# The second product for the state reads as seven block products, with a new order of all steps

## The chip, the cores and the metric

The kernel runs on one core of a Trainium2 chip. The metric is device time in microseconds (us) for one execution; lower is better. The core's engines run side by side and synchronise by semaphores: TensorE (matrix multiply; in the profile PE, with PEld for its weight loads), VectorE (DVE), ScalarE (ACT), GpSimd (POOL) and SyncE (SP, which here only issues DMA transfers). TensorE writes into PSUM, eight banks of 2 KB for each of 128 partitions; the other data lie in SBUF.

## What is computed

A cross attention between tokens and states, and a two-layer network on its result:

```python
# x: (8, 8, 512, 64) = (B, H, S, D); state: (8, 8, 32, 64)
a  = softmax(scale * x @ state^T);  xread = a  @ state     # tokens read states
a2 = softmax(scale * state @ x^T);  sread = a2 @ x         # states read tokens
attn = concatenate([xread, sread], axis=2)                  # (B, H, 512 + 32, D)
t = attn.transpose(0, 2, 1, 3).reshape(B * 544, 512)        # 4352 rows
h = t @ w_in                                                # w_in: (512, 2048)
g = maximum(h, 0) + alpha * minimum(h, 0)
out = g @ w_out                                             # w_out: (2048, 512), out: float32
```

Of the 544 output rows of each of the eight batch items 512 belong to tokens and 32 to states. The kernel calls the 8 x 32 = 256 state rows together "the reads" and gives them the item number 8.

## The kernel before

All matmuls are in float16 with float32 sums. The eight items of 512 tokens run one after the other, overlapped; the reads come at the end, because they need the attention of all items.

Every step is a token in one long list, ORDER, and a loop calls the step's function for each. Each engine runs its own instructions in the order in which the list issues them, so the list is the order of all engines. The tokens that matter (b is the item, 8 the reads):

- `F.b.jc.k`: first product, 128 of the 2048 columns of h, into PSUM bank k (0 to 5; two more banks form one larger buffer). For items 0 to 7 two matmuls with 512 columns, for the reads four with 256. `N.b.jc` is ScalarE's relu(-h), `G.b.jc` VectorE's multiply-add that makes g from it and h and so frees the bank.
- `S` and `O`: second product and its copy out for item 0, 16 matmuls of 128x512 for each 128 rows.
- `T`, `A`, `P`, `Q`: second product of items 1 to 7 by Strassen's scheme. The 512 tokens are cut into two halves r, the 2048 rows of w_out into two halves k, its 512 columns into two halves d. Seven products of blocks (`P.b.p.c.k`, p from 1 to 7, c a quarter of it) stand in place of eight. They need sums of blocks of w_out (`T`, once) and, in each item, of blocks of g: `A.b.i.grp.e`, four sums i in two groups of columns, on GpSimd (e = p), on VectorE (v) or by a DMA that adds (d, issued by GpSimd). Three chains of products accumulate in PSUM: p1, then 6, 7 and 4 on top of it; p2; and p5, then 3 on top of it. `Q.b.name.e` takes blocks out: p1, p5 and u are copies of a chain at some point of its way, c11, c12, c21 and c22 are blocks of the output.
- `M`, `MO`: product 2 of item 7 in three pieces, each with its own store.
- `R.q.jc2.k`, `RO.q.e`: second product of the reads. Two groups q of 128 rows, eight steps each, of two matmuls of 128x512, and a copy to SBUF.
- `W...`: a store, issued by SyncE. Stores and SyncE's other transfers start in the order of the list.
- `m`, `mo`, `rd`, `rdo`, `sc`, `sb`, `smax`, `ssh`, `sexp`, `ssum`, `snorm`, `wb`, `tx`, `te`, `tsum`, `tn`, `tt`: the attention. `rdo.b` copies the states' read of one item into the input of the reads' first product.

In the list of before the reads' second product begins while the last F steps are still going on, and its steps are spread over the last products of items 6 and 7:

```python
R.0.1 N.8.10 G.7.15 P.7.1.3 R.0.2 G.8.13 Q.7.p1.a A.7.1.1.d P.6.4.3 G.8.10 F.8.15.1 A.7.2.1.p
...
W.RO.0 M.7.2.0.3 R.1.7 Q.7.c21.a M.7.2.1 RO.1.a W.Q.7.c21 M.7.2.2 M.7.2.3 W.RO.1 MO.7.2.v W.MO.7.2
```

The functions `token_sum_of`, `product`, `token_cols`, `block_rows` and `product_out` already have branches for b == B (item 8) that the list of before doesn't reach: one tile of 128 rows in place of two, blocks of four items each as r, and `parts` in one small tile.

Of the kernel before, what the change touches and what calls it, by code (L numbers as in the profile page):

```python
# [9 lines left out]
F16 = mybir.dt.float16  # L10
# [40 lines left out]
xd.5 tn.3.0.a P.1.4.2 P.1.3.3 te.4.0 P.1.4.3 G.2.7 te.4.1 A.2.1.0.d F.2.15.0 Q.1.c12.v P.2.1.2
Q.1.c21.a A.2.3.1.p P.2.2.0.5 G.2.13 N.2.15 m.4.2 tn.3.1.a tsum.4 m.4.3.4.1 wb.3 P.2.2.1 mo.4.3.a.1
tt.3 P.2.1.3 mo.4.3.a.0 A.2.2.0.p G.2.15 P.2.2.2 mo.4.2.a.1 F.3.6.3 smax.4 W.Q.1.c12 F.3.15.1 N.3.6
P.2.2.3 W.Q.1.c21 mo.4.2.a.0 F.3.1.4 G.3.6 W.Q.1.c22 A.2.2.1.p Q.2.p1.a F.3.3.0 N.3.1 m.4.1
Q.2.c11.v N.3.15 F.3.7.3 G.3.1 P.2.6.0 W.Q.2.c11 mo.4.1.a.0 F.3.9.5 N.3.7 G.3.15 A.2.1.1.d P.2.6.1
N.3.3 G.3.7 ssh.p.4 F.3.0.4 P.2.6.2 G.3.3 N.3.0 P.2.5.0.1 N.3.9 G.3.0 F.3.8.3 mo.4.1.a.1 P.2.6.3
# [12 lines left out]
F.4.6.1 snorm.p.5 Q.3.p5.a F.4.13.3 mo.5.1.v.0 N.4.6 P.3.7.1 mo.5.1.a.1 G.4.8 P.3.3.0 N.4.13 P.3.7.2
G.4.6 A.4.3.0.p F.4.10.2 G.4.13 P.3.7.3 N.4.10 sc.6 Q.3.c22.v rd.4.5 wb.5 m.6.2.1.3 rdo.4.a P.3.3.1  # L70
mo.6.2.a.1 xd.7 P.3.4.0 mo.6.2.a.0 G.4.10 F.4.7.5 P.3.3.2 tx.6 A.4.2.0.p F.4.12.1 P.3.3.3 N.4.12
F.5.9.3 Q.3.c12.v ty.6 N.4.7 P.4.1.0.2 G.4.12 P.3.4.1 te.6.0 W.Q.3.c12 A.4.1.0.d P.4.1.1 G.4.7
te.6.1 tt.5 F.5.8.0 sb.6 P.3.4.2 N.5.9 A.4.3.1.p F.5.3.1 N.5.8 P.4.1.2 N.5.3 G.5.9 P.3.4.3 P.4.1.3
G.5.8 Q.3.c21.a F.5.10.5 A.4.2.1.p Q.4.p1.a smax.6 W.Q.3.c21 m.6.3 N.5.10 P.4.2.0.3 W.Q.3.c22
# [6 lines left out]
snorm.p.6 P.4.3.1 Q.4.c22.v N.5.15 F.5.6.4 W.Q.4.c22 G.5.15 P.4.3.2 N.5.6 P.4.4.0 G.5.4 te.7.0
P.4.3.3 A.5.1.0.d G.5.6 P.4.4.1 A.5.2.0.p m.7.2 Q.4.c12.v m.7.3.1.5 P.4.4.2 mo.7.3.a.1 tsum.7 wb.6
F.5.13.4 F.5.14.3 N.5.13 A.5.3.1.p P.5.1.1 mo.7.3.a.0 G.5.13 P.4.4.3 N.5.14 P.5.1.2 smax.7 F.6.3.1
P.5.2.0.5 N.6.3 F.6.10.4 G.5.14 ssh.p.7 Q.4.c21.a P.5.1.3 G.6.3 mo.7.2.a.1 P.5.2.1 N.6.10 F.6.7.3
Q.5.p1.v F.6.5.2 N.6.7 mo.7.2.v.0 A.5.1.1.d P.5.2.2 tn.7.1.a G.6.7 F.6.14.1 A.5.2.1.p tn.7.0.a
P.5.2.3 G.6.10 m.7.0 N.6.14 rd.6.3 tt.7 Q.5.c11.v sexp.7 P.5.6.0 G.6.14 A.5.4.0.p F.6.8.4 W.Q.5.c11
rdo.6.v P.5.6.1 N.6.8 W.Q.4.c21 F.6.6.5 G.6.8 P.5.6.2 W.Q.4.c12 N.6.6 P.5.5.0.1 A.5.4.1.p N.6.5
G.6.6 P.5.6.3 F.6.4.3 G.6.5 Q.5.u.a F.6.13.4 mo.7.0.a.0 ssum.7 P.5.5.1 N.6.13 P.5.7.0 P.5.5.2
F.6.2.5 G.6.13 snorm.p.7 P.5.7.1 mo.7.0.v.1 F.6.9.2 P.5.7.2 N.6.9 P.5.5.3 N.6.2 G.6.9 P.5.7.3
Q.5.p5.a F.6.11.4 G.6.2 N.6.4 m.7.1 rd.7.2 wb.7 P.5.3.0 rdo.7.a N.6.11 F.6.0.5 G.6.4 P.5.3.1  # L90
mo.7.1.a.1 Q.5.c22.v F.8.6.2 A.6.3.1.p P.5.3.2 G.6.11 N.8.6 F.6.1.3 N.6.0 G.8.6 P.5.4.0 mo.7.1.a.0
G.6.0 F.8.5.4 N.6.1 F.8.2.2 G.6.1 P.5.3.3 N.8.2 F.6.12.5 G.8.2 A.6.3.0.p P.5.4.1 Q.5.c12.v N.6.12
# [22 lines left out]
def kernel(  # L115
# [50 lines left out]
    live = {}  # L166
# [653 lines left out]
```

## Time and profile before

| | |
|---|---|
| time, median of 3 runs | 213.17 us (211.84 to 213.94) |
| the profiled execution | 213.67 us, of which the span from its first to its last instruction 211.8 us |
| mean granted TensorE clock | 0.987 |
| busy: TensorE, VectorE, ScalarE, GpSimd | 202.6, 174.0, 146.1, 170.3 us |
| DMA | 27.09 MB, mean 128 GB/s |

In the lines below, PE is a TensorE matmul, PEld a weight load, DVE VectorE, ACT ScalarE, POOL GpSimd, SPq the queue of transfers that SyncE issues and ACTq that of ScalarE. L655 is line 655 of the kernel: the matmul in `product`; L515 and L524 are the first products, L565 the step G, L547 N, L632 the sum in `token_sum_of`, L686, L690 and L693 the three ways out in `product_out`, L704 and L715 the pieces M and MO, L756 and L766 the reads' second product and its copy, L575 a store. A group line gives the operation, output and inputs with their sizes, the count, busy time in us and the mean in ns of one, and then the idle time of the engine ahead of it and what ended that.

### The profile page before, as it was taken

Reading aid. Unit: us, or ns where it says so; the run is one execution under the profiler, and the core shown is the slowest. Engines: PE = TensorE matmul, PEld = TensorE weight load, DVE = VectorE, ACT = ScalarE, POOL = GpSimd, SP = SyncE. Lnnn points to the kernel's source line nnn. Section 1 sums busy time; section 2 is a strip of 40 time slices with the busy share of each in tenths; the row PEclk is TensorE's granted clock in tenths of the full one; section 3 lists DMA queues with packets and bytes.
Section 4 is the critical chain, followed back from the end, with each engine's and each line's share of the span. In section 5 each row is a group of like instructions: output and inputs, shape, how many; then the busy total and the mean of one; then the engine's idle time right before and its main releaser. Section 6 shows DMA issues by size and latency. Waiting matters only on the chain.

```text
span 211.8 us, 5045 instructions
## 1 busy us (share of the span) xinstructions
PE 202.6 (96%) x2004; PEld 134.0 (63%) x2004; DVE 174.0 (82%) x268; ACT 146.1 (69%) x292; POOL 170.3 (80%) x110
## 2 busy tenths in 40 slices
PE   7689999999999999999999999999999999999992
PEld 6555344444547775676667757766777777877871
DVE  1688998999999999999999999899889876743230
ACT  4188996699997899977987767769667785331002
POOL 7469958999999999998998999999847944499300
PEclk9789999999999999999999999999999999999998
DMA  6999999599958748372998764243900640046026
GB/s 146 175 204 206 207 201 168 54 174 241 203 100 176 125 78 250 58 93 94 189 167 137 159 157 99 53 99 58 194 3 0 160 88 3 0 119 183 0 87 211
DMA packets 44502, 27.09 MB, mean 128 GB/s; under 512 B 22064, under 2 KB 41920, under 8 KB 44480
## 3 DMA queue, kind: packets, MB, share of 16 engines
q0 software_dynamic: 14192, 12.03, 37.6%
q1 hardware_dynamic: 29872, 14.43, 29.4%
q10 hardware_dynamic: 416, 0.33, 0.5%
q8 instruction: 15, 0.25, 0.5%
q14 instruction: 7, 0.06, 0.1%
HBM read 17.31 MB, written 8.91 MB: 124 GB/s over the span
## 4 chain that ended last, share of the span: by engine, by line
PE 81%; DVE 4%; ACT 4%; POOL 4%; DMA 3%; issue 1%; POOLq 0%; ACTq 0%
PE p L655 38%; PE h L515 23%; PE o L581 5%; PE h L524 3%; PE o L756 3%; PE m_ps L482 3%; DVE gp L565 3%; DMA st<-in_state_dram 3%; POOL s L632 2%; PE sr_ps L457 2%; ACT m L504 2%; POOL gp L614 1%; PE sc L322 1%; PE st_ps L256 1%; PE o L704 1%
## 5 line engine op out<-in xcount | busy, mean ns | idle before, releaser
L547 ACT ACTIVATE neg<-h 128x512 f32<-128x512 f32 (+1 forms) x144 | 80.1, 598 | 29.6 <-PE h L515 18.8
L565 DVE SCALAR_TENSOR_TENSOR gp<-neg,oma_sb,h 128x512 f16<-128x512 f32 x128 | 89.5, 734 | 8.0 <-ACT neg L547 7.4
L515 PE MATMUL h<-aT,m 128*128 128x512 f16 x250 | 69.8, 379 | 0.4 <-DVE gp L565 0.3
L632 POOL TENSOR_TENSOR s<-gp,s 128x1024 f16<-128x1024 f16 x28 | 65.8, 2436 | 4.2 <-DVE gp L565 4.0
L655 PEld LDWEIGHTS <-gp 128*128 128x128 f16 x432 | 41.7, 98 | 17.2 <-issue 2.3
L632 POOL TENSOR_TENSOR s<-gp 128x1024 f16<-128x1024 f16 x14 | 32.9, 2350 | 12.0 <-DVE gp L565 12.0
L655 PEld LDWEIGHTS <-s 128*128 128x128 f16 x336 | 31.9, 98 | 13.0 <-POOL s L632 1.6
L655 PE MATMUL p<-ws,s 128*128 128x256 f16 x224 | 33.7, 273 | 0.3 <-POOL s L632 0.2
L655 PE MATMUL p<-ws,gp 128*128 128x256 f16 x224 | 33.6, 273 | 0.0
L515 PEld LDWEIGHTS <-m 128*128 128x128 f16 x250 | 23.9, 98 | 13.5 <-issue 2.2
L504 ACT CAST m<-m_ps 128x512 f16<-128x512 f32 x51 | 28.9, 613 | 4.0 <-PE m_ps L482 2.7
L655 PE MATMUL p<-w_out_sb,gp 128*128 128x256 f16 x208 | 30.3, 273 | 0.0
L367 POOL TENSOR_TENSOR ts<-ts,mx 128x1024 f32<-128x1024 f32 (+1 forms) x9 | 17.1, 1899 | 7.0 <-DVE mx L361 7.0
L383 POOL TENSOR_TENSOR an<-ts,r 128x1024 f16<-128x1024 f32 (+1 forms) x9 | 16.7, 1853 | 2.3 <-DVE r L378 2.3
L581 PE MATMUL o<-w_out_sb,gp 128*128 128x512 f16 x64 | 16.8, 380 | 0.1
L655 PE MATMUL p<-w_out_sb,s 128*128 128x256 f16 x112 | 16.8, 273 | 0.0
L614 POOL DMA_DIRECT2D gp<-gp x14 | 13.6, 972 | 0.4 <-POOL s L632 0.3
L690 ACT COPY c<-p 128x512 f32<-128x512 f32 x6 | 3.5, 582 | 14.3 <-PE p L655 14.3
L482 PE MATMUL m_ps<-w_in_sb,stT 64*32 64x512 f16 x256 | 12.0, 384 | 0.1
L420 ACT ACTIVATE e<-sc,nb 128x512 f16<-128x512 f32 x16 | 11.0, 694 | 0.5 <-issue 0.5
L693 DVE TENSOR_TENSOR c<-p,p 128x512 f32<-128x512 f32 x13 | 8.9, 682 | 2.6 <-PE p L655 2.3
L581 PEld LDWEIGHTS <-gp 128*128 128x128 f16 x64 | 5.8, 97 | 8.1 <-issue 1.6
(73 smaller groups left out, 248.2 us busy)
## 6 DMA issues: line engine op xcount, KB each, us to landing
out_dram<-c SPq DMA_DIRECT2D x27, 256.0 KB, 2.8
xg<-in_x_dram POOLq DMA_DIRECT2D x7, 512.0 KB, 6.9
gp<-gp POOLq DMA_DIRECT2D x14, 256.0 KB, 4.2
w_in_sb<-in_moe_w_in_dram POOLq DMA_DIRECT2D x4, 512.0 KB, 11.5
w_out_sb<-in_moe_w_out_dram POOLq DMA_DIRECT2D x4, 512.0 KB, 12.8
out_dram<-osb SPq DMA_DIRECT2D x4, 256.0 KB, 4.0
out_dram<-osr SPq DMA_DIRECT2D x2, 256.0 KB, 2.5
x<-in_x_dram SPq DMA_DIRECT2D x1, 256.0 KB, 3.3
```

Source lines behind the costliest of these rows:

```text
L367: engine(e).tensor_tensor(ts, ts, over_blocks(cols(live["mx", b], j, S // N)), ALU.subtract)
L383: engine(e).tensor_tensor(blocks(cols(live["an", b], j, S)), blocks(cols(live["ts", b], j, S)), over_blocks(cols(live["r1", b], j, S // N) ...
L420: nc.scalar.activation(live["e2", b][:, g, :, :], live["sc", b][:, :, :, g, :].rearrange("p r j s -> p (r j) s"), EXP, bias=live["nb", b][ ...
L482: nc.tensor.matmul(t[N * k : N * (k + 1), :], st_head(b, h)[64 * r : 64 * r + 64, :], w_in_sb[64 * r : 64 * r + 64, c, 512 * f : 512 * (f ...
L504: copier(e)(m_tile(b)[:, f, g, :], live["mp", b, f][g])
L515: nc.tensor.matmul(h.rearrange("p (r j s) -> p r j s", r=2, j=2), ms[b][:, f, g, 128 * j : 128 * (j + 1)], weights(b, g), start=(g == 0), ...
L547: nc.scalar.activation(neg, h, RELU, bias=0.0, scale=-1.0)
L565: nc.vector.scalar_tensor_tensor(gt, negs.pop((b, jc)), oma_sb[:, jc : jc + 1], h, ALU.mult, ALU.add)
L581: nc.tensor.matmul(outs[b, q], token_cols(b, jc, q), w_out_sb[:, jc, :], start=(jc == 0), stop=(jc == n_jc - 1),)
L614: nc.gpsimd.dma_start(gp[:, 1, 0], gp[:, 1, 1], accum_op=ALU.add)
L632: engine(e).tensor_tensor(t, x, y, op)
L655: nc.tensor.matmul(chains[chain][:, t, :], lhs, rhs[:, i, :], start=(opens and i == 0 and t == 0), stop=(i == half_k - 1), skip_group_chec ...
```

## The change

The tokens R and RO are gone. The reads take the scheme of items 1 to 7 with half the width: `P.8.1` to `P.8.7` (28 steps of two matmuls of 128x256), eight sums `A.8` of 128x512 elements (six on VectorE, A.8.4.0 and A.8.4.1 on GpSimd), seven steps `Q.8` of 128x256, and four stores of 128 KB in place of two of 256 KB. The last of them, c12 of the reads, is issued by ScalarE's queue through a new token WA.

The list is the same up to `S.0.2.5` (196 tokens) and another from there on: F, N, G, P, A, Q, M and the attention stand in another order, in other banks, and some copies have changed between ScalarE and VectorE (27 `mo`, `Q`, `O` and `rdo` steps in one direction or the other, and three `tn` steps between GpSimd and ScalarE). The number of F, P (items 1 to 7), M, m, rd and sc steps is the same. The last F steps now come ahead of all products of the reads, and the end of the list mixes those with products of item 7:

```diff
-W.RO.0 M.7.2.0.3 R.1.7 Q.7.c21.a M.7.2.1 RO.1.a W.Q.7.c21 M.7.2.2 M.7.2.3 W.RO.1 MO.7.2.v W.MO.7.2
...
+A.7.3.0.p P.6.7.2 A.8.3.0.v N.7.4 P.6.2.0.4 G.7.11 F.7.5.1 P.6.7.3 G.7.4 N.7.5 P.6.2.1 A.8.1.0.v
+A.7.1.0.d P.7.1.0.2 Q.6.c22.v P.6.3.0 A.7.2.0.p P.6.2.2 G.7.5 W.Q.6.c22 F.7.12.3 A.8.3.1.v P.6.3.1
+N.7.12 P.7.1.1 A.7.3.1.p G.7.12 P.8.1.0.1 P.6.4.0 P.6.2.3 P.7.1.2 Q.6.c11.v P.8.1.1 P.6.3.2
+A.8.1.1.v W.Q.6.c11 P.8.1.2 A.7.1.1.d P.7.1.3 A.8.2.0.v A.7.2.1.p P.6.3.3 Q.7.p1.a P.6.4.1 Q.6.c12.v
+M.7.1.0.3 P.8.2.0.4 P.6.4.2 P.8.2.1 P.8.1.3 P.6.4.3 A.8.4.0.p P.7.6.0 Q.6.c21.v P.7.5.0.5 A.7.4.0.p
+Q.8.p1.v M.7.1.1 P.7.6.1 P.8.2.2 M.7.0.0.0 P.8.6.0 P.7.6.2 P.8.2.3 M.7.1.2 A.7.4.1.p P.7.6.3
+Q.8.c11.v M.7.0.1 A.8.2.1.v W.Q.8.c11 Q.7.u.a P.8.6.1 M.7.1.3 M.7.0.2 MO.7.1.v P.7.5.1 W.Q.6.c12
+P.7.7.0 W.Q.6.c21 A.8.4.1.p P.8.6.2 P.7.5.2 W.MO.7.1 P.8.5.0.4 P.8.6.3 P.7.7.1 Q.8.u.a P.7.5.3
+P.8.7.0 Q.7.p5.v P.7.7.2 M.7.0.3 P.8.5.1 P.7.7.3 M.7.2.0.3 P.8.7.1 Q.7.c22.v P.8.5.2 M.7.2.1 P.7.3.0
+MO.7.0.v W.Q.7.c22 P.8.5.3 M.7.2.2 P.7.4.0 Q.8.p5.a W.MO.7.0 P.8.7.2 M.7.2.3 P.7.3.1 MO.7.2.v
+P.7.4.1 W.MO.7.2 P.7.3.2 P.8.7.3 P.7.4.2 Q.8.c22.v P.7.3.3 W.Q.8.c22 P.8.3.0 Q.7.c12.v P.8.4.0
+P.7.4.3 P.8.4.1 W.Q.7.c12 Q.7.c21.v P.8.3.1 P.8.4.2 P.8.3.2 P.8.4.3 W.Q.7.c21 P.8.3.3 Q.8.c21.a
+Q.8.c12.v W.Q.8.c21 WA.Q.8.c12
...
+    def store_by_scalar(*what):
+        nc.scalar.dma_start(*stores.pop(what))
...
-        t = sums[b, i, grp] = moe.tile(
-            [128, 4, half_s], F16, name=f"s{i}_{b}_{grp}", tag=f"s_{grp}", bufs=3
-        )
         if b == B:
-            t = sums[b, i, grp] = t[:, :, :128]
+            k = "sums", i in (2, 4)
+            if k not in live:
+                live[k] = att.tile([128, 2, 2, 4, 128], F16, name=f"s{i}_{b}", tag="ts", bufs=2)
+            t = live[k][:, i in (1, 4), grp]
+        else:
+            t = moe.tile(
+                [128, 4, half_s], F16, name=f"s{i}_{b}_{grp}", tag=f"s_{grp}", bufs=3
+            )
+        sums[b, i, grp] = t
+        if b == B:
             gp = live["gs"].rearrange("p (k g j) (r s) -> p r k g j s", k=2, g=2, r=2)[:, :, :, grp]
...
-        "W": store, "M": last_piece, "MO": last_piece_out,
+        "W": store, "WA": store_by_scalar, "M": last_piece, "MO": last_piece_out,
```

More of the change, by code (lines that the diff above doesn't have):

```diff
@@ L51 @@
[L51 to L56, printed above, removed]
@@ L69 @@
[L69 to L74, printed above, removed]
@@ L81 @@
[L81 to L92, printed above, removed]
```

119 lines of the change are left out of this document (67 added, 52 removed).

## The prediction

> **What bounds the kernel now.** I read the page first, then busy time by stage, then what TensorE waits for, and last the chain and the store queue at the end.
>
> ```profile
> span 211.8 us, 5045 instructions
> ...
> PE 202.6 (96%) x2004; PEld 134.0 (63%) x2004; DVE 174.0 (82%) x268; ACT 146.1 (69%) x292; POOL 170.3 (80%) x110
> ```
> ```profile
> 40.00:100.00 60.00, 59.55 (x635) 37.30 (x632) 58.30 (x83) 53.97 (x112) 58.63 (x35) 1.00 0.74 137
> 100.00:120.00 20.00, 20.00 (x219) 13.61 (x204) 19.36 (x29) 16.64 (x34) 18.45 (x12) 1.00 0.91 162
> 120.00:187.00 67.00, 67.00 (x647) 48.70 (x646) 57.99 (x88) 44.85 (x90) 52.64 (x29) 1.00 0.37 78
> 187.00:207.60 20.60, 20.54 (x167) 15.36 (x164) 7.12 (x14) 3.41 (x8) 10.21 (x7) 1.00 0.41 112
> 207.60:211.80 4.20, 0.00 (x0) 0.00 (x0) 0.26 (x1) 0.23 (x1) 0.00 (x0) 0.74 0.59 208
> ```
> ```profile
> PE p L655 <- POOL s L632: 0.2, 1, 0.2
> PE h L515 <- ACT osb L748: 0.2, 1, 0.2
> ```
>
> In the second fence the columns are the stretch, its length, busy time of PE, PEld, DVE, ACT and POOL, the clock, the DMA engines' busy share and GB/s. From 40 us to the last product TensorE idles 0.5 of 167.6 us (59.55 of 60 and 20.54 of 20.6, the rest full) at clock 1.00. The third fence is everything that TensorE waited for after 40 us: two waits, 0.4 us together. A busy TensorE can still be a slow one, so the rate is needed; the chain of waits gives it, because there a run of matmuls stands with its true length:
>
> ```profile
> 182.25 3.06 PE p L655 x28
> ...
> 202.32 0.86 PE o L756 x4
> ```
> ```profile
> 207.20 0.35 PE o L704 x6
> 207.55 0.02 issue
> 207.57 0.29 DVE osb L715
> ```
>
> One 128x256 product matmul takes 3.06/28 = 0.109 us and one 128x512 matmul 0.86/4 = 0.215: cost goes with columns, and no gap is left for another order to close. So TensorE's amount of work sets the end up to 207.55, and after that the stores do. Two other facts matter: VectorE idles only 2.3 us between 40 and 120 (58.30 of 60, 19.36 of 20), so it is nearly a second bound there; from 187 on it is busy a third of the time.
>
> **The products of the reads.** Removed: 16 steps R of two 128x512 matmuls, 32 x 0.215 = 6.88 us. Added: seven products of eight 128x256 matmuls, 56 x 0.109 = 6.10. Every other TensorE step (F, P for items 1 to 7, M, m, rd, sc) is in both lists in the same number. TensorE: -0.78 us, all of it on the path.
>
> **What the blocks need besides.** Eight sums of 128x512 f16 (six on VectorE, two on GpSimd) and seven evictions of 128x256 for two of 128x512. No f16 sum on VectorE is in this trace. Near rows:
>
> ```profile
> L565 DVE SCALAR_TENSOR_TENSOR gp<-neg,oma_sb,h 128x512 f16<-128x512 f32 x128 | 89.5, 734 | 8.0 <-ACT neg L547 7.4
> ...
> L632 POOL TENSOR_TENSOR s<-gp,s 128x1024 f16<-128x1024 f16 x28 | 65.8, 2436 | 4.2 <-DVE gp L565 4.0
> ...
> L547 ACT ACTIVATE neg<-h 128x256 f32<-128x256 f32 x16 | 6.2, 386 | 8.3 <-PE h L524 8.3
> ...
> L565 DVE SCALAR_TENSOR_TENSOR gs<-neg,oma_sb,h 128x256 f16<-128x256 f32 x16 | 7.4, 478 | 2.8 <-ACT neg L547 2.8
> ...
> L693 DVE TENSOR_TENSOR c<-u,p 128x512 f32<-128x512 f32 x7 | 4.8, 683 | 1.6 <-PE p L655 1.6
> ...
> L313 DVE COPY xT<-xT_ps 128x512 f16<-128x512 f16 x7 | 2.6, 406 | 1.1 <-PE xT_ps L308 1.1
> ...
> L383 POOL TENSOR_TENSOR an<-ts,r 128x512 f16<-128x512 f32 x2 | 2.1, 1050 | 0.6 <-DVE r L378 0.6
> ...
> L715 DVE TENSOR_TENSOR osb<-p,o 128x256 f32<-128x256 f32 x1 | 0.4, 422 | 0.0
> ```
>
> The f16 copy gives 0.41, the f32 sum 0.68; I take 0.5 between them, nearer to the row with the same type: 6 x 0.5 = 3.0 us on VectorE, 2.4 to 4.1 by the ends. The Trainium skill (VectorE: DVE Perf Modes, "The perf-mode tier table") has tensor_tensor on 16-bit SBUF data at twice the f32 rate, 1224 ns for 2048 elements; that makes an estimate of 0.42 for 512, and 2.5 us in sum. No run here shows it.
>
> Three of the six sums stand in the list ahead of the last first-product's G (the step G.7.12), three behind it. What comes behind lies in the stretch from 187 on, where VectorE is free two thirds of the time. There I went through each wait that the blocks add, as TensorE steps between the last matmul that an eviction reads and the first that overwrites its bank:
> - u of the reads (ScalarE): the four matmuls each of P.7.7.1 and P.7.5.3, 8 x 0.109 = 0.87 us, against 0.39 for a 256-wide ScalarE pass. The tightest.
> - c22 of the reads (VectorE): ten matmuls, 1.09 us, against 0.42.
> - p1 of the reads: as much as 21 matmuls of 256 columns, 2.3 us, against 0.42 and a c21 of item 6 (0.68) queued ahead on VectorE.
> - GpSimd: its two sums (1.05 each) stand before A.7.4.0 and behind A.7.4.1. Between the place of A.7.4.1 and the first product that reads it lie 8.6 us of TensorE steps, against 2.4 for the sum itself and 3.5 (one sum of each kind) queued ahead.
>
> All are covered with 0.4 us or more to spare, so I cost them at zero. Should the tightest be held up by other ScalarE work, each eviction of 0.6 us queued ahead of it would cost TensorE 0.39 + 0.6 - 0.87 = 0.1 us.
>
> **The end.** Columns: start, length.
>
> ```profile
> 205.68 0.55 SPq L575 DMA_DIRECT2D out_dram<-c  x1
> ...
> 206.27 0.61 SPq L575 DMA_DIRECT2D out_dram<-osr  x1
> ...
> 207.31 0.54 SPq L575 DMA_DIRECT2D out_dram<-c  x1
> ...
> 207.94 0.58 SPq L575 DMA_DIRECT2D out_dram<-osr  x1
> 208.62 0.54 SPq L575 DMA_DIRECT2D out_dram<-osb  x1
> ```
> ```profile
> out_dram<-osr SPq DMA_DIRECT2D x2, 256.0 KB, 2.5
> ...
> out_dram<-osb SPq DMA_DIRECT2D x2, 64.0 KB, 2.1
> out_dram<-osb SPq DMA_DIRECT2D x1, 128.0 KB, 1.9
> ...
> st<-in_state_dram ACTq DMA_DIRECT2D x1, 64.0 KB, 2.6
> ```
> ```profile
> 0.72 0.43 ACTq L194 DMA_DIRECT2D st<-in_state_dram  x1
> ```
>
> Before, the last piece is ready at 207.57 + 0.29 = 207.86, but SyncE is issuing the store ahead of it and starts on it at 208.62: 0.76 us lost. The span ends 211.80 - 207.55 = 4.25 us behind the last matmul.
>
> After, call the end of the last matmul T. The last two evictions are c12 of the reads on VectorE (T + 0.02 + 0.42 = T + 0.44) and c21 on ScalarE (last matmul at T - 0.22, ready at T + 0.19). SyncE still has c21 of item 7: its last matmul ends at T - 1.3, twelve narrow matmuls before T, VectorE ends its 0.68 at T - 0.6 and SyncE its issue at about T. So c21 of the reads is issued at T + 0.2, and c12 goes on ScalarE's queue, which has nothing else left, at T + 0.46 instead of behind it at T + 0.8. Before, the last issue was at 208.62 - 207.55 = T + 1.07: 0.6 us later. The last store is now 128 KB (1.9) for 64 KB (2.1), behind another of 128 KB. A store by ScalarE's queue isn't in the trace; its issue of a load took 0.43, less than SyncE's 0.54. I take -0.5, with ends of 0 and -0.76. The Trainium skill (DMA: Bandwidth & Descriptors, "Issuing engines are not separate DMA queues") says that issuing from several engines saves only the issuing time and that the transfers share the same 16 DMA engines; the 0.76 us here is such an issuing time, so by it too this is the most there is to win.
>
> **The new order.** The lists agree up to S.0.2.5; behind it all is rearranged. TensorE has at most its 0.4 us of waits to win. To lose there is more, on VectorE. I counted steps up to the place where TensorE's steps behind the shared start add up to 84 us (about 120 us in the span). The same number of G; after has one softmax maximum and one sum with its reciprocals more, two state-read copies more, one output copy and two copies of m fewer:
>
> ```profile
> L504 DVE CAST m<-m_ps 128x512 f16<-128x512 f32 x13 | 8.7, 680 | 0.1
> ...
> L361 DVE TENSOR_REDUCE mx<-ts 128x32 f32<-128x1024 f32 x7 | 8.5, 1211 | 0.0
> ...
> L377 DVE TENSOR_REDUCE r<-ts 128x32 f32<-128x1024 f32 x7 | 8.4, 1206 | 0.2 <-ACT ts L373 0.2
> ...
> L378 DVE RECIPROCAL r<-r 128x32 f32<-128x32 f32 x7 | 2.5, 353 | 0.2
> ...
> L430 DVE RECIPROCAL r<-r 128x2 f32<-128x2 f32 x8 | 1.3, 158 | 0.1
> ...
> L468 DVE CAST XS<-sr_ps 128x128 f16<-128x128 f32 x2 | 0.9, 440 | 0.0
> ```
>
> 1.21 + 1.21 + 0.35 + 0.16 + 0.88 - 3 x 0.68 = +1.8 us, into 2.3 us of idle time. It fits, barely. Idle time that lies ahead of where the work arrives can't be used, and G then comes late to free one of the six banks that F opens, so TensorE waits. I take +0.4 us, ends -0.4 (both waits gone) and +1.8 (none of the idle time of use). From there to 187 after has about 3.6 us more on VectorE (three sums, one G and four of the reads' G at 0.46, three more evictions, one copy; one softmax part fewer) against 9.0 idle: nothing.
>
> **Sum.** -0.78 - 0.5 + 0.4 = -0.9 us. The profiled execution took 213.67 (span 211.8 and 1.9 around it), so 212.8 for such a one; it lies 0.5 above the median, 213.17, which gives **212.3**.
>
> **Rivals.**
> (a) VectorE becomes the bound. If none of its idle time between the shared start and 187 is of use, the 1.8 and 3.6 us both go onto TensorE: 213.2 - 1.3 + 5.4 = 217.3; with the first part alone and half of the second, 215.5. It decides once the additions up to 120 pass 2.3 us or arrive in lumps that hold up the F banks. For it: 96 to 97% busy there. Against: before, VectorE runs as dense and TensorE waits for no G after 40; and the new list takes up a bank behind an F no sooner than the old (the closest are 1.7 us of TensorE steps apart in both, 15 of 127 against 16 of 127 lie under 2.2).
> (b) The end gives nothing: the reads' 256 KB now go out last, with rows half as long, and a store by ScalarE's queue lands later by half a microsecond (the load of 64 KB there took 2.6, stores of 64 KB by SyncE 2.1). -0.78 + 0.4: 212.8. For it: the DMA engines are already 59% busy over the last 4.2 us. Against: the store that ended last, before, had waited 0.76 us for SyncE alone.
> (c) Everything turns out well: -0.78 - 0.76 - 0.4 = 211.2. Half of this case would read as faster by over 1%, because runs of one kernel differ by as much (211.84 to 213.94).
>
> **Chances.** Forecast 0.45, (b) 0.15, (c) 0.22, (a) 0.18. About 1% (2.1 us) is what a measurement of this kernel can tell from no change. Faster by over 1% (below 211.0): half of (c) and a part of the forecast from the spread of runs, 0.20. Slower (above 215.3): most of (a), 0.15. Within: 0.65. Range 210.7 to 215.3: below, (c) with some spread; above, the end of the unknown in the order (+1.8 for +0.4: 213.7) and the lower part of (a).
>
> **What would show it.** TensorE's matmuls of L756 gone and 56 more on L655; the last matmul at 206.8 to 207.5; its waits behind 40 us under 1 us in sum, if any on VectorE's G; the f16 sums at 0.4 to 0.7; the span's end 3.6 to 4.0 us behind the last matmul. Waits of TensorE above 2 us between 60 and 130 would prove (a); an end 4.2 us or more behind the last matmul, (b).

## The result and the profile after

The change makes the kernel slower. Six runs of the new kernel have a median of 217.97 us (217.24 to 219.27), six of the kernel before 213.56 (211.84 to 216.53). The ratio, which leaves disturbed runs out, is 1.0244 with an interval from 1.0208 to 1.0281. The forecast was 212.3, in a range up to 215.3.

The page of the profile after first (the execution took 217.42 us as a whole):

```profile
span 215.6 us, 5114 instructions
...
PE 202.6 (94%) x2028; PEld 136.4 (63%) x2028; DVE 185.4 (86%) x282; ACT 145.2 (67%) x290; POOL 171.2 (79%) x111
```

The lines of the program have moved by a few numbers: L667 is now the matmul in `product`, L518 and L527 the first products, L568 the step G, L644 the sum in `token_sum_of`, L698, L702 and L705 the ways out in `product_out`, L716 and L727 M and MO, L507 the copy `mo`, L423 the exponential `te`, L460 `rd`, L578 a store by SyncE, L581 the one that ScalarE issues (in the lines of before L581 is the step S).

TensorE is as long busy as before and the span is 3.8 us longer, so TensorE waits. VectorE is busy for 11.4 us more than before (174.0), although the change brings it some 3 us of sums and a few evictions. These two lines already say where to look. Next, everything that TensorE waits for from the place where the two lists part (about 34 us) to the end; the columns are the waiting line, what it waits for, us in total, times, and the longest:

```profile
PE p L667 <- DVE c L705: 1.5, 1, 1.5
PE sr_ps L460 <- DMA e2T<-e: 1.2, 1, 1.2
PE h L518 <- DVE gp L568: 0.6, 1, 0.6
PE sc L325 <- ACT m L507: 0.5, 1, 0.5
PE p L667 <- DVE s L644: 0.4, 1, 0.4
PE p L667 <- ACT u L698: 0.4, 1, 0.4
PE m_ps L485 <- ACT e L423: 0.2, 1, 0.2
PE h L518 <- ACT XS L471: 0.2, 1, 0.2
```

Eight waits, 5.0 us, where before had two, 0.4 us. Each of them costs some 0.16 us more than it says, because the end of a matmul is modelled late. The timeline of TensorE shows it (start, length, and in brackets the idle time ahead):

```profile
194.02 0.60 PE L667 MATMUL p<-ws,gp 128*128 128x256 f16 x4
194.46 0.60 PE L667 MATMUL p<-ws,s 128*128 128x256 f16 x4
196.51 0.60 PE L667 MATMUL p<-ws,gp 128*128 128x256 f16 x4 [1.45 <-DVE c L705]
```

A group of four is told as 0.60 long, and the next starts 0.44 after it. So this wait is 196.51 - 194.46 - 0.44 = 1.61, not 1.45.

**One measure for all kernels.** The first 36 us vary from run to run, and there all lists are the same. I take the time from a mark in the shared part, the group of eight matmuls of S, to the end of the last matmul, which the chain of waits gives. It is read from one profile of each kernel. For before the chain shown in the prediction ends its matmuls at 207.55, and the mark is this row of TensorE's timeline:

```profile
37.22 1.89 PE L581 MATMUL o<-w_out_sb,gp 128*128 128x512 f16 x8
```

For after, the mark in the timeline, then the last row of the chain (start, length):

```profile
36.07 1.89 PE L587 MATMUL o<-w_out_sb,gp 128*128 128x512 f16 x8
```
```profile
207.45 4.60 PE p L667 x42
```

Before: 207.55 - 37.22 = 170.33. After: 212.05 - 36.07 = 175.98, which is 5.65 longer. Span: 1.15 less in the start, 5.65 more to the last matmul, 0.70 less behind it, in sum the 3.8 above. The start isn't the change's, and some of it is given back: where the mark comes early, the first of the eight waits to come (for the DMA that transposes e) is longer, 1.2 here and 0.3 in two other runs whose marks lie at 37.4.

### The profile page after: what moved, and what is told of

It is laid out like the page before. It is cut to its first block, busy times and chain, and to the rows that moved or that the text cites. A ratio compares the mean times of both kernels' runs of the same rounds, so it can differ in the third digit from the quotient of the medians.

```text
span 215.6 us, 5114 instructions
## 1 busy us (share of the span) xinstructions
PE 202.6 (94%) x2028; PEld 136.4 (63%) x2028; DVE 185.4 (86%) x282; ACT 145.2 (67%) x290; POOL 171.2 (79%) x111
## 4 chain that ended last, share of the span: by engine, by line
PE 64%; DVE 18%; ACT 6%; DMA 6%; issue 3%; POOL 2%; ACTq 0%; POOLq 0%; DVEq 0%
PE p L667 35%; PE h L518 20%; DVE gp L568 7%; DMA w_in_sb<-in_moe_w_in_dram 4%; DVE s L644 3%; PE m_ps L485 3%; PE h L527 3%; ACT m L507 2%; DMA e2T<-e 2%; ACT e L423 2%; DVE nb L408 2%; DVE m L507 2%; DVE ts L356 1%; DVE c L705 1%; PE sr_ps L460 1%
## 5 line engine op out<-in xcount | busy, mean ns | idle before, releaser
L550 ACT ACTIVATE neg<-h 128x512 f32<-128x512 f32 (+1 forms) x144 | 78.6, 589 | 28.7 <-PE h L518 21.5
L568 DVE SCALAR_TENSOR_TENSOR gp<-neg,oma_sb,h 128x512 f16<-128x512 f32 x128 | 89.1, 736 | 4.8 <-ACT neg L550 4.7
L518 PE MATMUL h<-aT,m 128*128 128x512 f16 x250 | 70.3, 379 | 1.2 <-DVE gp L568 0.9
L644 POOL TENSOR_TENSOR s<-gp,s 128x1024 f16<-128x1024 f16 x28 | 62.5, 2368 | 4.4 <-DVE gp L568 4.1
L667 PEld LDWEIGHTS <-gp 128*128 128x128 f16 x432 | 42.0, 98 | 16.3 <-issue 2.5
L667 PEld LDWEIGHTS <-s 128*128 128x128 f16 x368 | 35.0, 98 | 13.0 <-issue 2.0
L667 PE MATMUL p<-ws,s 128*128 128x256 f16 x248 | 37.2, 273 | 0.9 <-DVE s L644 0.4
L667 PE MATMUL p<-ws,gp 128*128 128x256 f16 x224 | 33.6, 273 | 1.5 <-DVE c L705 1.5
L518 PEld LDWEIGHTS <-m 128*128 128x128 f16 x250 | 23.4, 98 | 15.4 <-issue 3.3
L644 POOL TENSOR_TENSOR s<-gp 128x1024 f16<-128x1024 f16 x14 | 30.3, 2172 | 3.5 <-DVE gp L568 3.2
L507 ACT CAST m<-m_ps 128x512 f16<-128x512 f32 x53 | 30.1, 610 | 3.8 <-DVE m L507 2.6
L667 PE MATMUL p<-w_out_sb,gp 128*128 128x256 f16 x208 | 30.1, 273 | 0.0
L370 POOL TENSOR_TENSOR ts<-ts,mx 128x1024 f32<-128x1024 f32 (+1 forms) x9 | 15.9, 1767 | 8.1 <-DVE mx L364 8.1
L620 POOL DMA_DIRECT2D gp<-gp x14 | 12.7, 926 | 7.1 <-issue 6.3
L667 PE MATMUL p<-w_out_sb,s 128*128 128x256 f16 x120 | 18.2, 273 | 0.0
L423 ACT ACTIVATE e<-sc,nb 128x512 f16<-128x512 f32 x16 | 11.0, 689 | 3.9 <-DVE ts L356 2.1
L408 DVE TENSOR_REDUCE nb<-sc 128x2 f32<-128x1024 f32 x8 | 9.7, 1216 | 1.0 <-PE sc L325 0.9
L705 DVE TENSOR_TENSOR c<-p,p 128x512 f32<-128x512 f32 x13 | 8.9, 681 | 1.9 <-PE p L667 1.2
```

The source lines that it names most:

```text
L370: engine(e).tensor_tensor(ts, ts, over_blocks(cols(live["mx", b], j, S // N)), ALU.subtract)
L408: nc.vector.tensor_reduce(nb, live["sc", b].rearrange("p r j g s -> p g (r j) s"), AX.XY, ALU.max)
L423: nc.scalar.activation(live["e2", b][:, g, :, :], live["sc", b][:, :, :, g, :].rearrange("p r j s -> p (r j) s"), EXP, bias=live["nb", b][ ...
L507: copier(e)(m_tile(b)[:, f, g, :], live["mp", b, f][g])
L518: nc.tensor.matmul(h.rearrange("p (r j s) -> p r j s", r=2, j=2), ms[b][:, f, g, 128 * j : 128 * (j + 1)], weights(b, g), start=(g == 0), ...
L550: nc.scalar.activation(neg, h, RELU, bias=0.0, scale=-1.0)
```

## The experiments

Ten kernels. Times of the kernel before, in the same rounds, had medians from 212.19 to 212.65. "Mark to last matmul" is the measure just explained.

**Is it the new reads or the new order?** First the new reads in the old order: the list of before up to `G.8.14`, R and RO taken out, the block products put into the tail by hand, with all eight sums on VectorE behind `Q.7.p5.v`:

```diff
-W.RO.0 M.7.2.0.3 R.1.7 Q.7.c21.a M.7.2.1 RO.1.a W.Q.7.c21 M.7.2.2 M.7.2.3 W.RO.1 MO.7.2.v W.MO.7.2
...
+P.7.7.0 P.7.5.2 P.7.7.1 P.7.5.3 M.7.0.3 Q.7.p5.v A.8.3.0.v A.8.2.0.v P.7.7.2 M.7.2.0.3 P.7.7.3
+M.7.2.1 Q.7.c22.v P.7.3.0 A.8.3.1.v A.8.2.1.v W.Q.7.c22 P.8.6.0 P.8.6.1 A.8.1.0.v P.7.3.1 A.8.1.1.v
...
+P.8.4.1 P.8.3.2 P.8.4.2 W.Q.7.c21 P.8.4.3 P.8.3.3 Q.8.c21.a Q.8.c12.v W.Q.8.c21 WA.Q.8.c12
```

> The order of before up to P.6.3.2 and G.8.14, and the seven products of the reads in a tail written by hand: all eight f16 sums on VectorE behind Q.7.p5, where GpSimd has just ended its last sum. Theory 1: the sums take 0.4 to 0.5 us each, TensorE waits under 0.6 us behind 185, the last matmul ends near 206.9 and the span 3.6 us behind it: 212.3, 1.2 under before. Theory 3 (the new form of the reads costs more than it saves wherever it stands): 215 or more. Theory 2 (the order alone): also 212.3, so this run speaks against theory 3 only.

Measured: 211.12 us (median; 210.59 to 214.55), ratio 0.9941 [0.9906, 0.9976]: 0.6% faster than the kernel before, with an interval that lies below 1, and faster than the changed kernel. TensorE's waits from 34 us on, the sums' group rows, and the last row of the chain:

```profile
PE p L667 <- POOL s L644: 0.2, 1, 0.2
PE h L518 <- ACT osb L760: 0.2, 1, 0.2
```
```profile
L644 DVE TENSOR_TENSOR s<-gs,s 128x512 f16<-128x512 f16 x4 | 1.6, 420 | 0.1
L644 DVE TENSOR_TENSOR s<-gs 128x512 f16<-128x512 f16 x4 | 1.6, 416 | 0.0
```
```profile
202.57 4.38 PE p L667 x40
```

The waits are those of before, and its mark is at 37.22 too: 206.95 - 37.22 = 169.73, 0.60 less than before. The block products do what the sum said of them (0.78), and the loss isn't theirs.

Then the other way round, the new order with the reads as R and RO:

```diff
-S.0.2.5 F.1.1.0 S.0.0.6 mo.1.3.v.0 N.1.1 F.1.3.5 tn.1.1.a G.1.1 S.0.0.7 lx.3 sc.2 tt.1 O.0.0.a
...
+S.0.2.5 mo.1.3.a.0 F.1.1.0 rd.0.5 N.1.1 G.1.1 rdo.0.a lx.3 tn.1.1.a sc.2 F.1.5.5 tx.2 tt.1 F.1.9.0
```

> The changed kernel's order, with the reads' second product in its old form (16 steps R, no f16 sums of the reads, two evictions and two stores). Theory 1: the waits before 190 us stay (about 3 us: the first states' read for its transpose, first products for VectorE, two for ScalarE), those behind it go: 0.8 more TensorE work, 1.9 less waiting: 216.5 to 217. Theory 2 (all from the order): 218 or more. Theory 3 (all from the sums): 213.5.

Measured: 217.17 us (216.31 to 217.43), ratio 1.0205 [1.0140, 1.0269]. Mark to last matmul 173.22, 2.9 more than before, with the waits of after in the middle (0.7, 0.5, 0.4, 0.2, 0.2) but only 0.3 for the transposing DMA. Its mark lies at 37.41, as late as before's. So the order by itself costs about 3 us, and nearer to 4 when the start is early.

**The sums beside GpSimd.** The six sums on VectorE, by groups, after:

```profile
L644 DVE TENSOR_TENSOR s<-gs,s 128x512 f16<-128x512 f16 x2 | 5.2, 2586 | 0.0
L644 DVE TENSOR_TENSOR s<-gs 128x512 f16<-128x512 f16 x4 | 5.0, 1250 | 0.0
```

10.2 us where the kernel above needs 6 x 0.42 = 2.5. The timeline of VectorE and GpSimd in that stretch:

```profile
186.59 2.41 POOL L644 TENSOR_TENSOR s<-gp,s 128x1024 f16<-128x1024 f16 x1
...
187.61 3.75 DVE L644 TENSOR_TENSOR s<-gs 128x512 f16<-128x512 f16 x1
188.68 2.39 POOL L644 TENSOR_TENSOR s<-gp 128x1024 f16<-128x1024 f16 x1
191.28 0.73 DVE L568 SCALAR_TENSOR_TENSOR gp<-neg,oma_sb,h 128x512 f16<-128x512 f32 x1
...
192.54 0.41 DVE L644 TENSOR_TENSOR s<-gs 128x512 f16<-128x512 f16 x1
192.55 0.86 POOL L620 DMA_DIRECT2D gp<-gp  x1 [1.49 <-issue]
192.87 2.98 DVE L644 TENSOR_TENSOR s<-gs,s 128x512 f16<-128x512 f16 x1
193.16 2.40 POOL L644 TENSOR_TENSOR s<-gp,s 128x1024 f16<-128x1024 f16 x1
195.78 0.68 DVE L705 TENSOR_TENSOR c<-u,p 128x512 f32<-128x512 f32 x1
...
197.04 4.21 POOL L644 TENSOR_TENSOR s<-gp,s 128x1024 f16<-128x1024 f16 x2
...
199.34 2.19 DVE L644 TENSOR_TENSOR s<-gs,s 128x512 f16<-128x512 f16 x1
```

Each long sum ends 0.3 us behind GpSimd's: 187.61 + 3.75 = 191.36 and 188.68 + 2.39 = 191.07; 195.85 and 195.56; 201.53 and 201.25. A sum beside GpSimd's issue of a DMA (192.55) takes its 0.41. The multiply-adds of L568, which read h from PSUM, take 0.73 to 0.74 whatever GpSimd does. And because VectorE is in order, the eviction c12 of item 6 (195.78) stands behind the sum of 2.98, and TensorE's 1.45 behind that.

The theory: a VectorE sum with two inputs in SBUF doesn't run while GpSimd is in its own sums. The rivals: these sums are slow wherever they stand, or VectorE simply has too much to do. Three experiments part them. In the first, ScalarE copies one input of each of the six sums to PSUM (four copies for six sums), and nothing else is moved:

```diff
+        if b == B and e == "v":
+            c = live["cp"][:, grp].rearrange("p (j s) -> p j s", s=128)
+            a21, a22 = (a21, c) if i == 2 else (c, a22)
...
+            live["cp"] = two("cp", [128, 2, 512], F32)
...
+        nc.scalar.copy(
+            live["cp"][:, grp].rearrange("p (j s) -> p j s", s=128), gs[:, 1, k, grp]
+        )
```

> The changed kernel, but ScalarE first copies one operand of each of the six VectorE sums to PSUM (four copies), so that no VectorE sum has two inputs in SBUF. Theory 1 (a VectorE sum with two SBUF inputs can't run while GpSimd runs its own two-input sums): the six sums take 0.7 us each whatever GpSimd does, none over 1 us; TensorE's waits of 1.45 us near 196 and 0.44 near 201 go; time 216.0, 1.9 under the changed kernel. Theory 2 (the sums are late only because the new order is late as a whole): the sums keep durations of 2 us or more, or the waits move to the next step; time 217.5 to 218. Theory 3 (all of the loss comes from the sums): 213.

Measured: 216.87 us (214.89 to 219.13), ratio 1.0167 [1.0073, 1.0260]. The timeline:

```profile
191.11 2.42 POOL L647 TENSOR_TENSOR s<-gp,s 128x1024 f16<-128x1024 f16 x1
...
192.40 0.68 DVE L647 TENSOR_TENSOR s<-gs,cp 128x512 f16<-128x512 f16 x1
...
193.20 2.41 POOL L647 TENSOR_TENSOR s<-gp 128x1024 f16<-128x1024 f16 x1
194.86 0.68 DVE L647 TENSOR_TENSOR s<-cp,gs 128x512 f16<-128x512 f32 x1
```

All six take 0.68, three of them (at 192.40, 194.86 and 201.59) wholly in the midst of GpSimd's sums, and those of 128x1024 are no longer for it (2.40 to 2.42 here, 2.39 to 2.41 in after). The slower form (0.68 for 0.42) is the faster one there. Both waits of the tail are gone (TensorE is busy all the time from 190 to 210). Its profiled run has another wait, 2.36 us for the DMA that adds, at 67.20. The clock then stands at 0.50 until about 70, some 1.4 us more by estimate. So its mark to last matmul, 177.44, doesn't serve as a measure; without these two it would be about 173.5 by the same estimate, near the 173.82 of the next experiment.

The second experiment leaves after's order as it is to `G.7.12` and puts all eight sums behind `Q.7.p5.v`, where GpSimd has ended:

```diff
-A.7.3.0.p P.6.7.2 A.8.3.0.v N.7.4 P.6.2.0.4 G.7.11 F.7.5.1 P.6.7.3 G.7.4 N.7.5 P.6.2.1 A.8.1.0.v
+A.7.3.0.p P.6.7.2 N.7.4 P.6.2.0.4 G.7.11 F.7.5.1 P.6.7.3 G.7.4 N.7.5 P.6.2.1 A.7.1.0.d P.7.1.0.2
...
+W.Q.6.c12 P.7.7.0 W.Q.6.c21 P.7.5.2 W.MO.7.1 P.7.7.1 P.7.5.3 M.7.0.3 Q.7.p5.v A.8.3.0.v A.8.2.0.v
```

> The changed kernel with its order up to G.7.12 as it is, and all eight f16 sums of the reads on VectorE behind Q.7.p5, where GpSimd has ended its last sum; the products that read them come behind. Theory 1 (a two-input sum waits for GpSimd's port; order and sums each have their own share): the sums take 0.42 us each, the waits of 1.45 and 0.44 us go, those ahead of 190 us stay: about 2.1 under the changed kernel, 215.3. If the loss in the tail came from the order too (theory 2): 217 or more.

Measured: 215.55 us (214.98 to 215.95), ratio 1.0138 [1.0093, 1.0184]. The sums take 0.41 to 0.43 (414 to 425 ns), the waits for c and s are gone, the six others are there as before. Mark to last matmul 173.82, 2.16 less than after: what the two waits come to (1.45 + 0.44 + 2 x 0.16 = 2.2).

The third turns it round. In the good kernel (the old order with the new reads) one sum is moved to a place ahead of GpSimd's last row of sums:

```diff
-F.8.15.1 A.7.2.1.p P.8.2.0.5 N.8.15 P.7.6.0 G.8.15 F.8.12.0 Q.6.c21.v P.8.2.1 N.8.12 G.8.12 P.7.6.1
+F.8.15.1 A.7.2.1.p P.8.2.0.5 N.8.15 P.7.6.0 G.8.15 F.8.12.0 A.8.3.0.v Q.6.c21.v P.8.2.1 N.8.12
```

> The old order with the new reads, and one f16 sum (A.8.3.0, 0.42 us of work) ahead of Q.6.c21 on VectorE, where GpSimd runs sums back to back. Theory 1: this sum lasts until GpSimd's row of sums ends, 4 us or more; Q.6.c21 behind it and the piece M.7.1 that needs its bank are late; TensorE waits 3 us or more and the time is 214 or more. If a sum just shares the port: it lasts 0.5 to 1 us and the time stays at 211 to 212.

Measured: 218.21 us, one run. VectorE, GpSimd and TensorE in the timeline, and a stretch of the stages' table (length; PE, PEld, DVE, ACT, POOL busy; clock; DMA share; GB/s):

```profile
189.39 6.55 POOL L644 TENSOR_TENSOR s<-gp,s 128x1024 f16<-128x1024 f16 x3
...
189.83 6.40 DVE L644 TENSOR_TENSOR s<-gs 128x512 f16<-128x512 f16 x1
...
196.88 1.01 PE L716 MATMUL o<-w_out_sb,gp 128*128 128x128 f16 x8 [5.94 <-DVE c L702]
```
```profile
198.00:200.00 2.00, 2.00 (x11) 1.42 (x10) 0.64 (x2) 0.00 (x0) 0.00 (x0) 0.50 0.79 264
```

One sum of 0.42 us takes 6.40, to 0.29 behind the end of three GpSimd instructions in a row, and TensorE waits 5.94 us for the copy queued behind it. The clock is at 0.50 from 194 to 200, so TensorE runs at half speed for 3 us behind the wait: 11 matmuls start in the stretch shown, 21 in the 2 us after it. One moved token costs 7.4 us from the mark to the last matmul (177.14 for 169.73).

**The order.** Two kinds of wait are in after's middle. The first can be read in the timeline around 112 and 126 us:

```profile
110.78 1.25 DVE L356 STREAM_TRANSPOSE ts<-sc 128x1024 f32<-128x1024 f32 x1
...
112.06 0.69 ACT L423 ACTIVATE e<-sc,nb 128x512 f16<-128x512 f32 x1 [1.32 <-DVE ts L356]
...
112.74 0.58 ACT L698 COPY u<-p 128x512 f32<-128x512 f32 x1
...
113.36 0.60 PE L667 MATMUL p<-ws,s 128*128 128x256 f16 x4 [0.42 <-ACT u L698]
...
125.93 1.28 DVE L507 CAST m<-m_ps 128x512 f16<-128x512 f32 x2
126.64 0.58 ACT L507 CAST m<-m_ps 128x512 f16<-128x512 f32 x1 [1.33 <-DVE m L507]
```

ScalarE and VectorE read the same tile of two PSUM banks, one behind the other. ScalarE waits 1.3 us for VectorE's read of the scores and for its copy of m, and what stands behind ScalarE is late: u at 112.74, and then a product. At 46.64 it is VectorE that waits, for 1.08 us, and g of the first product is late by it. The waiting engine stands idle even before the other begins its read: in the last line ScalarE is idle from 125.31 and VectorE's copy starts at 125.93; at 46.64 VectorE is idle from 45.56 and ScalarE's copy starts at 45.99. So it waits for the instruction that stands ahead in the list, and not only while two reads would meet. Where the two halves of m lie in two tiles of one bank each, the copies overlap; the same timeline of before:

```profile
108.42 0.69 DVE L504 CAST m<-m_ps 128x512 f16<-128x512 f32 x1
108.87 0.58 ACT L504 CAST m<-m_ps 128x512 f16<-128x512 f32 x1
```

Before also has copies of m by both engines out of one tile, but 3 to 20 tokens apart in the list; behind the shared part of the list, five of after's six such pairs stand 1 or 2 apart. The experiment puts four of these five (3.1, 5.3, 6.1 and 6.2; not 7.2) on ScalarE alone, and the exponentials of items 4 and 6 ahead of VectorE's read, next to each other:

```diff
-mo.3.1.v.1 F.1.0.3 N.1.7 F.1.6.0 G.1.10 N.1.0 S.0.0.7 G.1.7 N.1.6 F.1.4.5 lx.4 S.0.1.6 sexp.2 G.1.0
+mo.3.1.a.1 F.1.0.3 N.1.7 F.1.6.0 G.1.10 N.1.0 S.0.0.7 G.1.7 N.1.6 F.1.4.5 lx.4 S.0.1.6 sexp.2 G.1.0
...
-A.2.3.0.p te.4.1 P.1.4.1 sb.4 P.1.3.3 N.2.7 W.Q.1.c22 P.1.4.2 te.4.0 tsum.3 P.2.2.1 G.2.4 P.2.1.0.1
+A.2.3.0.p te.4.1 te.4.0 P.1.4.1 sb.4 P.1.3.3 N.2.7 W.Q.1.c22 P.1.4.2 tsum.3 P.2.2.1 G.2.4 P.2.1.0.1
...
-N.4.5 m.6.2 P.3.7.1 N.4.7 W.Q.3.c11 G.4.5 P.3.3.0 N.4.6 A.4.3.0.p P.3.7.2 mo.6.2.v.1 mo.6.2.a.0
+N.4.5 m.6.2 P.3.7.1 N.4.7 W.Q.3.c11 G.4.5 P.3.3.0 N.4.6 A.4.3.0.p P.3.7.2 mo.6.2.a.1 mo.6.2.a.0
```

> The changed kernel; the two copies out of one two-bank PSUM tile are given to ScalarE both (m of 3.1, 5.3, 6.1, 6.2: one VectorE copy each became a ScalarE copy), and the two exponentials of items 4 and 6 both stand ahead of VectorE's transpose of the same tile. Theory 4 (two engines' reads of one PSUM tile run one behind the other, and what is queued behind the waiting engine is late): TensorE's waits at 48 (0.65, first product for VectorE), 113 (0.42, for ScalarE's u) and 127 us (0.54, scores for ScalarE's m) go, about 2 us in all with what the modelled ends hide: 215.4. If VectorE's amount of work were the bound there (my rival a): VectorE has 4 copies of 0.68 less, waits shrink by no more than that and sit in other places; 216 to 217.

Measured: 216.69 us (216.29 to 218.14), ratio 1.0205 [1.0139, 1.0272]. TensorE's waits that answer to it, besides the 1.4 and 0.4 of the sums, which stay:

```profile
PE m_ps L485 <- ACT m L507: 0.6, 1, 0.6
...
PE sr_ps L460 <- DMA e2T<-e: 0.3, 1, 0.3
...
PE h L518 <- DVE gp L568: 0.2, 1, 0.2
```

The waits at 113 and 127 are gone and that for g fell from 0.6 to 0.2, but ScalarE, which now has both copies, makes a new one of 0.6. Mark to last matmul is 1.79 less than after (174.19); 0.95 of that is the shorter wait for the DMA, which isn't the edit's. So the edit is worth about 0.84.

The other kind is that DMA. In before's list four S steps, three F steps and the scores `sc.2` stand between the mark and `rd.0`, in after's one F step; its input, transposed by a DMA issued at 35.49, lands at 39.62. The experiment puts three S steps ahead of it, and leaves `sc.2` behind it:

```diff
-S.0.2.5 mo.1.3.a.0 F.1.1.0 rd.0.5 N.1.1 G.1.1 rdo.0.a lx.3 tn.1.1.a sc.2 F.1.5.5 tx.2 tt.1 F.1.9.0
-T.1.1.p N.1.5 S.0.2.6 N.1.9 sb.2 S.0.3.5 ty.2 S.0.2.7 te.2.1 S.0.3.6 G.1.5 te.2.0 T.2.1.p S.0.3.7
+S.0.2.5 mo.1.3.a.0 F.1.1.0 N.1.1 G.1.1 S.0.2.6 S.0.3.5 S.0.2.7 rd.0.5 rdo.0.a lx.3 tn.1.1.a sc.2
+F.1.5.5 tx.2 tt.1 F.1.9.0 T.1.1.p N.1.5 N.1.9 sb.2 ty.2 te.2.1 S.0.3.6 G.1.5 te.2.0 T.2.1.p S.0.3.7
```

> The changed kernel with the first states' read (rd.0) three second-product steps of item 0 later, which come ahead of it instead. If the 1.2 us that TensorE waited there for the transpose by DMA lie on its path: the wait is 0.3 us or less and the time 217.0. If VectorE is the bound of that stretch: the wait goes and first products wait for VectorE that much longer; time 218.

Measured: 217.11 us (216.88 to 217.47), ratio 1.0214 [1.0141, 1.0288]. The wait for the DMA is 0.5 in place of 1.2, but a new one of 1.06 for VectorE's g stands at 43.33. Nothing is won (mark to last matmul 176.49, 0.5 more than after): the wait has moved to the engine that is next late. Why can be read from VectorE's timeline and the first product behind it:

```profile
40.26 1.22 DVE L408 TENSOR_REDUCE nb<-sc 128x2 f32<-128x1024 f32 x1 [1.46 <-PE sc L325]
...
42.56 0.71 DVE L568 SCALAR_TENSOR_TENSOR gp<-neg,oma_sb,h 128x512 f16<-128x512 f32 x1
...
43.33 0.59 PE L518 MATMUL h<-aT,m 128*128 128x512 f16 x2 [1.06 <-DVE gp L568]
```

VectorE is idle for 1.46 us until the scores come, which TensorE makes behind `rd.0`; then two attention steps of 1.2 us each stand ahead of the multiply-add that frees the bank. In after the same multiply-add is as late behind the scores, but ten matmuls of S cover it; here four are left there, because six have moved ahead of `rd.0`. In before the scores come first (40.83, and `rd.0` at 42.57). That order wasn't tried in the new list.

**All together.** The moved sums and the reads on one engine:

```diff
-mo.3.1.v.1 F.1.0.3 N.1.7 F.1.6.0 G.1.10 N.1.0 S.0.0.7 G.1.7 N.1.6 F.1.4.5 lx.4 S.0.1.6 sexp.2 G.1.0
+mo.3.1.a.1 F.1.0.3 N.1.7 F.1.6.0 G.1.10 N.1.0 S.0.0.7 G.1.7 N.1.6 F.1.4.5 lx.4 S.0.1.6 sexp.2 G.1.0
...
-A.7.3.0.p P.6.7.2 A.8.3.0.v N.7.4 P.6.2.0.4 G.7.11 F.7.5.1 P.6.7.3 G.7.4 N.7.5 P.6.2.1 A.8.1.0.v
+A.7.3.0.p P.6.7.2 N.7.4 P.6.2.0.4 G.7.11 F.7.5.1 P.6.7.3 G.7.4 N.7.5 P.6.2.1 A.7.1.0.d P.7.1.0.2
```

> The changed kernel with both repairs: the f16 sums behind GpSimd's last sum, and reads of one two-bank tile by one engine (or with the exponentials ahead). If the two causes are separate and add up: 2.1 less for the sums, 0.9 less for the tiles, 214.4; TensorE's waits left are the first states' read for its transpose (0.3 to 1.2) and one for a ScalarE copy near 52 (0.6). If they overlap: 215 to 215.5.

Measured: 214.32 us (213.81 to 215.34), ratio 1.0113 [1.0076, 1.0150]. Mark to last matmul 172.82: 3.16 less than after. The wait for the DMA is 0.17 shorter here; the other 2.99 are what the sums (2.16) and the reads (0.84) gave alone. The two causes add up. Then these two and the later `rd.0` (the diffs above):

> As new_order_both, and the first states' read three second-product steps later. Alone, that step moved TensorE's wait to first products (VectorE's G 1.7 us) and won nothing. If that was because VectorE's copy of m stood behind ScalarE's there, which new_order_both has removed: 1 us under new_order_both, 213.4, waits behind 34 us 1.2 in sum. If VectorE's work itself is late there: as new_order_both, 214.4.

Measured: 215.60 us (214.03 to 216.97), ratio 1.0167 [1.0098, 1.0236]. Mark to last matmul 172.98, the same as without the third edit (172.82). The wait for the DMA is gone and one of 1.0 for g stands in its place. The list still loses 3.25 us against the old order (169.73) with all three edits.

**The last store's queue.** In the good kernel the last store goes to SyncE:

```diff
-P.8.4.1 P.8.3.2 P.8.4.2 W.Q.7.c21 P.8.4.3 P.8.3.3 Q.8.c21.a Q.8.c12.v W.Q.8.c21 WA.Q.8.c12
+P.8.4.1 P.8.3.2 P.8.4.2 W.Q.7.c21 P.8.4.3 P.8.3.3 Q.8.c21.a Q.8.c12.v W.Q.8.c21 W.Q.8.c12
```

> The old order with the new reads, the last store on SyncE's queue in place of ScalarE's. By the prediction's sum the issue waits for the store ahead: about 0.3 us later, span end 3.8 to 3.9 us behind the last matmul in place of 3.5. If the transfers set the end: no change.

Measured: 215.63 us, one run, with a wait of 2.1 us at 115.28 for another item's transposing DMA, which the edit doesn't touch; so it is read from its end alone. There the last matmul ends at 209.99 and the span at 213.9, 3.9 later; with ScalarE's queue it is 206.95 and 210.5, 3.55 later. ScalarE's queue is worth 0.35 us in these two profiles.

## Why the prediction was wrong

Two terms failed: the sums on VectorE, put at nothing, cost 2.2 us, and the new order, put at +0.4, cost 3 to 4. The other two came out near what was worked out.

**TensorE's products: right.** -0.78 was taken, -0.60 measured in the old order, where the waits are the same 0.4.

**The end: right.** -0.5 was taken with ends of 0 and -0.76, and 4.25 - 3.55 = 0.70 came. After's last instructions:

```profile
211.85 0.37 ACT L702 COPY c<-p 128x256 f32<-128x256 f32 x1 [4.87 <-PE p L667]
212.07 0.42 DVE L705 TENSOR_TENSOR c<-parts,p 128x256 f32<-128x256 f32 x1 [0.62 <-PE p L667]
212.53 0.65 ACTq L581 DMA_DIRECT2D out_dram<-c  x1
```

The last store is issued 0.04 behind its eviction, 0.48 behind the last matmul (212.05), as worked out (T + 0.46). Its issue takes 0.65; the prediction, from the 0.43 of a load, had expected less than SyncE's 0.54. Rival (b) falls.

**The sums on VectorE: a cost put at nothing.** The prediction said "All are covered with 0.4 us or more to spare, so I cost them at zero." They cost 2.16 us, and by none of the four waits that the prediction had listed: TensorE waits for an eviction of item 6 that is queued behind a sum, and for a sum itself. The duration of one was right where GpSimd stands still (0.41 to 0.43 measured, 0.5 taken). The estimate of 0.42 that the prediction drew from the Trainium skill (VectorE: DVE Perf Modes, "The perf-mode tier table") agrees with it. What failed is the check: I asked whether each eviction's engine is free for as long as its instruction lasts, and took the sum's length as the same everywhere. I counted GpSimd's work only as a chain of its own, not as what VectorE would have to stand aside for, and three of the six sums (3.75, 2.98 and 2.19 us above) lie just where GpSimd makes the last sums of item 7. "VectorE is free two thirds of the time" there was a fact of an engine with no such instruction in it: the trace of before has no f16 sum on VectorE, as the prediction itself said.

The Trainium skill has this rule, and the prediction left it out: GPSIMD Engine Reference, "8. Key points", tells of contention with VectorE instructions that have two SBUF inputs, and SBUF — State Buffer, "SBUF: two separate sides", of an exclusive lock that whichever starts first has for the whole instruction. The traces agree that VectorE's sum stands still, and go further than one instruction: 6.40 us across three of GpSimd's. On who goes first they don't agree: the sum at 192.87 is recorded as starting 0.29 us ahead of GpSimd's (193.16), and is held up all the same.

**The new order: mis-sized.** The prediction took +0.4 with an end of +1.8. The list alone cost 2.9 us (new order, old reads) and up to 4.1 (173.82 - 169.73, where the start was early, and with it the wait for the DMA 0.9 longer). Its method was to compare amounts of work, and by it VectorE was to be the engine in danger. VectorE was not denser than before (19.36 of 20 from 100 to 120 us), but less:

```profile
100.00:120.00 20.00, 19.58 (x169) 13.35 (x168) 18.39 (x27) 15.43 (x32) 18.54 (x12) 1.00 0.70 129
```

What TensorE loses are waits for another engine at single places, which no amount shows. One kind is shown by its experiment: two engines' reads of one tile brought next to each other, 0.84 us. The other, `rd.0` and behind it the scores brought to another place, is argued from the traces, because the experiment only moved its wait. In a kernel where TensorE has 0.4 us of waits in 168, any such place falls on the path.

**Rival (a): nearest in time, but not by its mechanism.** It was to give 215.5 to 217.3 by VectorE's work, and 217.97 came, 0.7 above; its proof was waits of over 2 us between 60 and 130. There are 0.42 and 0.54. Its phrase that additions might "arrive in lumps" is nearest to what happened, but neither place nor cause was named.

**What the sum comes to.** From mark to last matmul after has +5.65: the block products -0.6, the sums beside GpSimd +2.16, the order the rest, 4.1. By the waits: 5.0 - 0.4 = 4.6 and six more modelled ends at 0.16, 1.0, less the 0.6, make 5.0. Some 0.65 us stands in no row.

**What stays open.** Whether GpSimd holds up the sum for its two inputs in SBUF or for its faster f16 form: the form with an input in PSUM differs in both (0.68 for 0.42). Two rows of after speak for the inputs: f16 copies out of PSUM, as fast as the sum (0.41), keep their time (three of them within 1.05 us from 15.65, beside a GpSimd instruction of two inputs from 15.71 to 16.77), and a VectorE transpose with one f16 input in SBUF keeps its 1.25 (at 35.94, beside a GpSimd sum from 35.86 to 37.98). A sum of two SBUF inputs in the slower form isn't in these kernels. Why the two reads of one two-bank tile go one behind the other: that the wait begins before the other engine's read speaks for the program, but whether the program or the chip asks for it wasn't tried apart. Whether the scores ahead of `rd.0`, as in before, would end the waits near 40. And a part of what the order still loses with two causes removed (172.82 - 169.73 = 3.1 us): its waits (1.0, 0.6 and four of 0.2, with their modelled ends, less those of the old order) explain 2.6.

## What to carry to other kernels

An instruction's duration belongs to its neighbours as well: before VectorE is given a sum of two SBUF operands, look what GpSimd does in that stretch, and put the sum behind GpSimd's row of instructions or, as here, take one operand from PSUM. When a whole list is reordered under a full TensorE, equal amounts of work say little; check for each pair of engines that read one tile, and each step fed by a DMA, how far apart they stood before and stand now, and what a step moved there takes along behind it. And a new scheme is best tried in the old order first: here that separates a gain of 0.6% from a loss of 2.4%.

## What the runs showed of the hardware that was not expected

- A VectorE f16 sum of 128x512 with both operands in SBUF takes 0.42 us alone and 2.19, 2.98, 3.75 and 6.40 beside GpSimd's sums; it ends 0.3 us behind the last of GpSimd's instructions that follow on each other, not behind the first. The profile counts all of it as busy.
- With one operand in PSUM the same sum takes 0.68 at any time, and GpSimd's issue of a DMA (0.87) doesn't hold up the form with two SBUF operands (0.41 and 0.42).
- The granted clock fell to 0.50 in the course of or just behind TensorE waits of 2.14 us (last_store_syncE, at 115.28), 2.36 (sum_from_psum, at 67.20) and 5.94, and stayed there until 3 to 5 us behind the wait's end; the waits of up to 1.6 us in after left it at 1.00.
- The wait for the same transposing DMA at the same place of after's list was 0.3, 0.3, 1.0, 1.2, 1.2 and 1.3 us in six profiles, the two short ones where the mark came latest. In the old order TensorE waits for it in none of four profiles.
